# Attention in 64x64 tiles of the PE array, q and k transposed by DMA, and w_out matmuls 14 slots behind those of w_in

## The chip, the core and the metric

The kernel runs on one core of a Trainium2 chip. Its engines work side by side, each on its own instruction stream: TensorE (PE, matmuls, with a weight-load part PEld), VectorE (DVE), ScalarE (ACT), GpSimd (POOL) and SyncE (SP). Matmul results go to PSUM, which has eight banks of 512 float32 columns; everything else lies in SBUF. DMAs are issued here by POOL (loads) and by SP (stores). The metric is the device time of one execution in microseconds (us); lower is better.

## What is computed

```python
# q, k, v: (8 batches, 8 heads, 576 tokens, 64)
scores = q @ k.T / sqrt(64), only where |i - j| <= 32
attn = softmax(scores);  a = attn @ v
x = a.transpose(0, 2, 1, 3).reshape(4608, 512)
h = x @ w_in                      # w_in 512 x 2048
g = where(h >= 1, h, where(h <= -1, 0, (h + 1)**2 / 4))
out = g @ w_out                   # w_out 2048 x 512, out float32
```

Inputs are float32; the kernel works in bfloat16 and sums in float32.

## The kernel before

**Order.** The order of the instructions is written out by hand. A prelude computes the first half of batch 0's attention. Then one loop of 152 slots (index `a`, `t` the block of 256 tokens, `f` one of eight pieces of 256 columns of w_in) carries the rest. A slot holds, on PE, eight matmuls of 256 columns with w_in (L359, result `hp`); ACT then computes `rr` (L363), DVE `tensor_max` in place in `hp` (L364) and the product `gT` (L365), which together are the activation. `hp` has two PSUM banks. Four matmuls of 512 columns with w_out (L375, result `op`) follow for the block before, eight slots behind; every fourth slot an `op` bank is finished, copied by ACT to `osb` (L379) and stored by SP (L381). Slots 0 to 7 have no w_out matmuls, slots 144 to 151 nothing but them.

**Attention in the slots.** Heads go in pairs: head y in partitions 0 to 63, head y+4 in 64 to 127; there are four such pairs a batch, 32 in all (index `i`). A dictionary `ev` says which piece of attention sits in which slot. `relay` (L171) reorders a loaded q; `tpose` transposes q or k on PE (L187) and copies the result out of PSUM, for q to `qT` (L200, ACT), for k into the block-diagonal buffer `kz` (L194, mostly DVE, partly ACT in the first slots). `kz` holds, for each chunk of 64 keys, the two heads' columns in separate halves with zeros elsewhere, so that one full 128x128 matmul computes both heads. `scores` runs nine such matmuls for an index in three groups (L220), takes the exponential on ACT (L224) and multiplies by the window mask on DVE (slots below 16) or POOL (L225). `pv` runs twice for an index, for 288 queries each: row sums with a block-diagonal matrix of ones (`dn`, L238 and L239), products with block-diagonal `vz` (`nm`, L248), then reciprocal as Ln and Exp on ACT (L252, L253); the product of both (L257, DVE) writes `xT`, the operand of the w_in matmuls, at the beginning of the next slot (`flush`).

**Loads.** All loads are issued by POOL and cast float32 to bfloat16. For q rows of 2,304 bytes are read (L100); for k (from the third double pair on) and v pieces of 256 bytes (L95, L105), one double pair (`m`, two indices) at a time. The prelude issues the loads of the first three double pairs and all weights; those of the fourth and later stand at the head of given slots. A load waits for the eighth load before it in this queue.

Of the kernel before, what the change touches and what calls it, by code (L numbers as in the profile page):

```python
# [8 lines left out]
FP = mybir.dt.float32  # L9
# [6 lines left out]
def kernel(  # L16
# [15 lines left out]

    nc = tc.nc
    B, H, S, D = q.shape
    NT, DM, DFF = out.shape[0], 512, 2048
    NP = B * H // 2
    NC = S // 64
    HALF = S // 2

    def qrange(c):  # L40
        return max(0, 64 * c - 32), min(S, 64 * c + 96)


    GROUPS = [(0, 2, 4), (1, 3), (6, 8, 5, 7)]
    pcol, PW = {}, 0
    for c in (1, 3, 0, 2, 4, 6, 8, 5, 7):
        pcol[c] = PW
        PW += qrange(c)[1] - qrange(c)[0]

    def pc(c, qq):  # L50
        return pcol[c] + qq - qrange(c)[0]

    const = ctx.enter_context(tc.tile_pool(name="const", bufs=1))
    qkn = ctx.enter_context(tc.tile_pool(name="qkn", bufs=3))
    qjp = ctx.enter_context(tc.tile_pool(name="qjp", bufs=2))
    qtp = ctx.enter_context(tc.tile_pool(name="qtp", bufs=3))
    ptp = ctx.enter_context(tc.tile_pool(name="ptp", bufs=4))
# [11 lines left out]
    ones2 = const.tile([128, 128], BF, name="ones2")  # L69
    mask1 = const.tile([128, 128], BF, name="mask1")  # L70
    maskp = const.tile([128, PW], BF, name="maskp")
    w_in = const.tile([128, 4, DFF], BF, name="w_in")
    w_out = const.tile([128, 16, DM], BF, name="w_out")
    zrow = const.tile([128, 2 * S], BF, name="zrow")
    xT = const.tile([128, 4, NT], BF, name="xT")
    kz = [const.tile([128, NC, 2, 64], BF, name=f"kz{i}") for i in range(6)]
    vz = [const.tile([128, 2, NC, 128], BF, name=f"vz{i}") for i in range(4)]

    ctx.enter_context(tc.manual_schedule())


    qn, kn = {}, {}

    LONG = 2

    def load_qk(m):
        b, qd = divmod(m, 2)
        for src, dst, nm in ((q, qn, "qn"), (k, kn, "kn")):  # L90
            if nm == "kn" and m >= LONG:
                t = dst[m] = qkn.tile([128, NC, 2, D], BF, name="kn", tag="kn")
                for g in range(2):
                    for h in range(2):
                        nc.gpsimd.dma_start(out=t[64 * g:64 * g + 64, :, h],  # L95
                                            in_=src[b, 2 * qd + g + 4 * h].rearrange("(c r) d -> r c d", r=64))
                continue
            t = dst[m] = qkn.tile([128, 2, S], BF, name=nm, tag=nm)
            rows = src[b].rearrange("(h y) s d -> h (y s) d", h=2)[:, 2 * qd * S:2 * qd * S + 2 * S]
            nc.gpsimd.dma_start(out=t, in_=rows.rearrange("h (x j) d -> x h (j d)", j=NC))  # L100

    def load_v(m):
        b, qd = divmod(m, 2)
        for h in range(2):
            nc.gpsimd.dma_start(  # L105
                out=vz[m % 4][64 * h:64 * h + 64, :, :, 64 * h:64 * h + 64].rearrange("r g c d -> r (g c) d"),
                in_=v[b, 4 * h + 2 * qd:4 * h + 2 * qd + 2].rearrange("g (c r) d -> r (g c) d", r=64))
# [7 lines left out]
    def load_w_out(n):  # L115
        nc.gpsimd.dma_start(out=w_out[:, 8 * n:8 * n + 8],
                            in_=moe_w_out.rearrange("(ko ki) f -> ki ko f", ki=128)[:, 8 * n:8 * n + 8])

    nc.scalar.preload_act_table_set("natural_log_exp_and_others")
    load_qk(0)  # L120
# [9 lines left out]
    load_qk(1)  # L130

    def vz_off(n, h):
        return vz[n][64 * h:64 * h + 64, :, :, 64 * (1 - h):64 * (1 - h) + 64].rearrange("r g c d -> r (g c) d")

    nc.vector.memset(zrow, 0.0)
    for n in range(2):
        for h in range(2):
            nc.scalar.copy(vz_off(n, h), zrow[64 * h:64 * h + 64].rearrange("r (c d) -> r c d", d=64))
    for t in kz:
        for h in range(2):  # L140
            nc.vector.memset(t[64 * h:64 * h + 64, :, 1 - h], 0.0)
    nc.vector.memset(ones2, 0.0)
    for h in range(2):
        nc.vector.memset(ones2[64 * h:64 * h + 64, 64 * h:64 * h + 64], 1.0)
    for cs in ((0,), (2, 4, 6), (8,), (1, 3), (5, 7)):
        q0, q1 = qrange(cs[0])
        j0 = q0 - (64 * cs[0] - 32)
        n = len(cs)
        nc.vector.tensor_copy(
            maskp[:, pcol[cs[0]]:pcol[cs[0]] + n * (q1 - q0)].rearrange("p (n j) -> p n j", n=n),  # L150
            mask1[:, j0:j0 + q1 - q0].rearrange("p (n j) -> p n j", n=1).to_broadcast([128, n, q1 - q0]))
    load_v(0)
    load_v(1)
    load_w_in(0, 512)
    load_w_in(512, DFF)
    for n in (2, 3):
        for h in range(2):
            nc.gpsimd.memset(vz_off(n, h).bitcast(FP), 0.0)
    load_qk(2)
    load_v(2)  # L160
    load_w_out(0)
    load_w_out(1)


    qj, kj, qT, kT = {}, {}, {}, {}

    def relay(m, t, eng):

        src, dst, nm = ((qn, qj, "qj"), (kn, kj, "kj"))[t]
        dst[m] = qjp.tile([128, NC, 2, D], BF, name=nm)  # L170
        eng.tensor_copy(dst[m].rearrange("p j h d -> p h j d"),  # L171
                        src[m].rearrange("p h (j d) -> p h j d", d=D))

    TJ = [(0, 5), (5, 9)]

    def tpose(m, t, early=False):

        nat = t >= 2 and m >= LONG
        src = qj if t < 2 else kn if nat else kj
        dst = qT if t < 2 else kT  # L180
        j0, j1 = TJ[t % 2]
        if t % 2 == 0 and not nat:
            dst[m] = qtp.tile([128, 2, S], BF, name="qT" if t < 2 else "kT")
        pool, tag = (ps_h, "hp") if early else (ps_s, "sc")
        ps = pool.tile([128, 5, 128], BF, name="tp", tag=tag)
        for j in range(j0, j1):
            nc.tensor.transpose(ps[:, j - j0], src[m][:, j].rearrange("p h d -> p (h d)"), ident)  # L187
        n = j1 - j0
        if nat:
            for g in range(2):  # L190
                for h in range(2):
                    r = slice(64 * h, 64 * h + 64)
                    copy = nc.scalar.copy if m < 4 and h else nc.vector.tensor_copy
                    copy(kz[2 * (m % 3) + g][r, j0:j1, h],  # L194
                                          ps[r, :n].rearrange("d c (g r) -> d g c r", g=2)[:, g])
            return
        o = dst[m].rearrange("d g (p j) -> d g p j", j=NC)[:, :, :, j0:j1]
        i = ps[:, :n].rearrange("d j (g p) -> d g p j", g=2)
        if t < 2 or t == 3:
            nc.scalar.copy(o, i)  # L200
        else:
            nc.vector.tensor_copy(o, i)

    def zfill(m, g, early=False):
        for h in range(2):
            r = slice(64 * h, 64 * h + 64)
            copy = nc.gpsimd.tensor_copy if not early else nc.scalar.copy if h else nc.vector.tensor_copy
            copy(kz[2 * (m % 3) + g][r, :, h], kT[m][r, g].rearrange("d (c r) -> d c r", r=64))

    pt = {}  # L210

    def scores(i, g, eng):
        m, gg = divmod(i, 2)
        if g == 0:
            pt[i] = ptp.tile([128, PW], BF, name="pt")
        ps = ps_s.tile([128, 512], FP, name="sc", tag="sc")
        off = 0
        for c in GROUPS[g]:
            q0, q1 = qrange(c)
            nc.tensor.matmul(ps[:, off:off + q1 - q0], kz[2 * (m % 3) + gg][:, c].rearrange("d h r -> d (h r)"),  # L220
                             qT[m][:, gg, q0:q1], start=True, stop=True)
            off += q1 - q0
        seg = slice(pcol[GROUPS[g][0]], pcol[GROUPS[g][0]] + off)
        nc.scalar.activation(pt[i][:, seg], ps[:, :off], AF.Exp, scale=D ** -0.5)  # L224
        eng.tensor_mul(pt[i][:, seg], pt[i][:, seg], maskp[:, seg])  # L225

    def pv(i, hf, spare=False):
        lo, hi = HALF * hf, HALF * hf + HALF
        if spare:
            dn = ps_o.tile([128, HALF], FP, name="dn", tag="op")  # L230
            nm = ps_o.tile([128, HALF], FP, name="nm", tag="op")
        else:
            dn = ps_d.tile([128, HALF], FP, name="dn")
            nm = ps_n.tile([128, HALF], FP, name="nm")
        odd = (1, 3) if hf == 0 else (5, 7)
        e0 = pc(2 * hf * 2, lo) if hf else pc(0, 0)
        o0, o1 = qrange(odd[0])[0], qrange(odd[1])[1]
        nc.tensor.matmul(dn, ones2, pt[i][:, e0:e0 + HALF], start=True, stop=False)  # L238
        nc.tensor.matmul(dn[:, o0 - lo:o1 - lo], ones2, pt[i][:, pcol[odd[0]]:pcol[odd[0]] + o1 - o0],  # L239
                         start=False, stop=True)  # L240
        parts = []
        for c in list(range(0, NC, 2)) + list(range(1, NC, 2)):
            q0, q1 = qrange(c)
            q0, q1 = max(q0, lo), min(q1, hi)
            if q0 < q1:
                parts.append((c, q0, q1))
# [58 lines left out]
    TB = 256  # L305
# [115 lines left out]
```

## Time and profile before

Three runs took 357.29, 357.70 and 357.76 us, median 357.70. The profiled execution took 357.66 us, of which the profile's span is 355.8; about 1.9 us lie outside the span.

| | busy, us | share of the span | instructions |
|---|---|---|---|
| PE | 322.8 | 91% | 2752 |
| PEld | 233.0 | 65% | 2752 |
| DVE | 272.8 | 77% | 513 |
| ACT | 227.7 | 64% | 455 |
| POOL | 166.5 | 47% | 211 |

| groups | count | mean, ns |
|---|---|---|
| hp matmul, 256 columns (L359) | 1152 | 275 |
| op matmul, 512 columns (L375) | 576 | 379 |
| sc / dn / nm matmuls (L220, L238 and L239, L248) | 288 / 128 / 320 | 220 / 285 / 215 |
| transposes on PE (L187) | 288 | 236 for q |
| rr on ACT (L363) | 144 | 596 |
| hp, gT on DVE (L364, L365) | 144 each | 699, 687 |
| exp on ACT (L224), 480 / 352 / 256 columns | 32 each | 564 / 459 / 379 |
| mask on POOL (L225), 480 / 352 / 256 columns | 26 / 24 / 24 | 1094 / 874 / 682 |
| Ln, Exp of the sums (L252, L253), 288 columns | 64 each | 414, 444 |
| kz copies on DVE (L194), 320 / 256 columns | 52 / 52 | 319 / 286 |
| xT on DVE (L257), 288 columns | 64 | 455 |
| osb copy on ACT (L379) | 36 | 586 |

Matmuls are pipelined: the mean of one is its latency, longer than its distance from the next, so a matmul's price is read from the starts of a run of them. In the timeline a row is a run of like instructions: start, length, engine, line, operation, operands and count. In the table of stages each engine's busy time in the stage is followed by its number of instructions; the last three numbers are the granted clock, the DMA share and GB/s. A line of the waits reads: engine and line, what it waited for, us in total, times, longest. A line of the chain: start, length, what it was.

### The profile page before, as it was taken

Reading aid. Unit: us, or ns where it says so; the run is one execution under the profiler, and the core shown is the slowest. Engines: PE = TensorE matmul, PEld = TensorE weight load, DVE = VectorE, ACT = ScalarE, POOL = GpSimd, SP = SyncE. Lnnn points to the kernel's source line nnn. Section 1 sums busy time; section 2 is a strip of 40 time slices with the busy share of each in tenths; the row PEclk is TensorE's granted clock in tenths of the full one; section 3 lists DMA queues with packets and bytes.
Section 4 is the critical chain, followed back from the end, with each engine's and each line's share of the span. In section 5 each row is a group of like instructions: output and inputs, shape, how many; then the busy total and the mean of one; then the engine's idle time right before and its main releaser. Section 6 shows DMA issues by size and latency. Waiting matters only on the chain.

```text
span 355.8 us, 7157 instructions
## 1 busy us (share of the span) xinstructions
PE 322.8 (91%) x2752; PEld 233.0 (65%) x2752; DVE 272.8 (77%) x513; ACT 227.7 (64%) x455; POOL 166.5 (47%) x211
## 2 busy tenths in 40 slices
PE   1768197878999999999999999999999999999995
PEld 1647174655777777777777777777777776666662
DVE  7549368676888888888888888888888787887770
ACT  6977366676777777777777777777766654444441
POOL 8946393068494849494949494942423300000000
PEclk9989889999999999999999999999999999999999
DMA  7999999059693939393939393930000000010011
GB/s 106 185 201 193 185 169 133 2 60 101 64 88 74 88 72 91 71 89 71 91 71 96 65 98 64 97 65 31 31 31 31 29 30 31 31 59 29 32 46 72
DMA packets 83809, 28.24 MB, mean 79 GB/s; under 512 B 71488, under 2 KB 78656, under 8 KB 83776
## 3 DMA queue, kind: packets, MB, share of 16 engines
q0 software_dynamic: 78592, 18.36, 56.3%
q1 hardware_dynamic: 5184, 9.44, 7.1%
q8 instruction: 21, 0.34, 0.4%
q14 instruction: 12, 0.10, 0.1%
HBM read 36.70 MB, written 9.44 MB: 130 GB/s over the span
## 4 chain that ended last, share of the span: by engine, by line
PE 79%; DMA 8%; DVE 5%; POOL 3%; ACT 3%; issue 2%; ACTq 0%; POOLq 0%
PE op L375 33%; PE hp L359 32%; DMA qn<-in_q_dram 4%; DMA w_in<-in_moe_w_in_dram 4%; PE nm L248 4%; PE tp L187 3%; PE sc L220 3%; PE dn L238 2%; PE dn L239 2%; DVE hp L364 1%; DVE gT L365 1%; DVE kz L194 1%; POOL vz L105 1%; ACT rr L363 1%; ACT kz L194 1%
## 5 line engine op out<-in xcount | busy, mean ns | idle before, releaser
L359 PE MATMUL hp<-xT,w_in 128*128 128x256 bf16 x1152 | 151.7, 275 | 1.6 <-DVE gT L365 1.2
L375 PE MATMUL op<-w_out,gT 128*128 128x512 bf16 x576 | 146.5, 379 | 0.0
L363 ACT ACTIVATE rr<-hp 128x512 f32<-128x512 f32 x144 | 85.8, 596 | 72.7 <-PE hp L359 69.8
L364 DVE TENSOR_TENSOR hp<-hp,rr 128x512 f32<-128x512 f32 x144 | 100.7, 699 | 40.9 <-ACT rr L363 38.0
L359 PEld LDWEIGHTS <-w_in 128*128 128x128 bf16 x1152 | 109.2, 99 | 21.6 <-DVE gT L365 1.9
L225 POOL TENSOR_TENSOR pt<-pt,maskp 128x480 bf16<-128x480 bf16 (+2 forms) x74 | 65.6, 889 | 101.9 <-ACT pt L224 101.7
L365 DVE SCALAR_TENSOR_TENSOR gT<-rr,hp 128x512 bf16<-128x512 f32 x144 | 98.9, 687 | 4.9
L375 PEld LDWEIGHTS <-gT 128*128 128x128 bf16 x576 | 53.0, 98 | 37.2
L224 ACT ACTIVATE pt<-sc 128x352 bf16<-128x352 f32 (+2 forms) x96 | 44.3, 468 | 0.7 <-PE sc L220 0.6
L95 POOL DMA_DIRECT2D kn<-in_k_dram x56 | 41.8, 775 | 1.0 <-DVE qj L171 0.9
L257 DVE TENSOR_TENSOR xT<-nm,rc 128x288 bf16<-128x288 f32 x64 | 29.0, 455 | 14.1 <-ACT rc L253 12.3
L220 PE MATMUL sc<-qT,kz 128*128 128x128 bf16 (+1 forms) x288 | 30.9, 220 | 5.5 <-ACT pt L224 4.3
L252 ACT ACTIVATE lr<-dn 128x288 f32<-128x288 f32 x64 | 26.5, 414 | 13.7 <-PE dn L239 13.6
L194 DVE COPY kz<-tp 64x320 bf16<-64x320 bf16 (+1 forms) x104 | 31.4, 302 | 2.8 <-ACT kz L194 1.8
L200 ACT COPY qT<-tp 128x640 bf16<-128x640 bf16 (+1 forms) x32 | 23.5, 741 | 12.7 <-PE tp L187 9.7
L105 POOL DMA_DIRECT2D vz<-in_v_dram x32 | 28.3, 897 | 4.8 <-DMA w_out<-in_moe_w_out_dram 2.9
L253 ACT ACTIVATE rc<-lr 128x288 f32<-128x288 f32 x64 | 28.4, 444 | 2.0
L187 PE MATMUL tp<-ident,qj 128*128 128x128 bf16 x144 | 14.4, 236 | 16.8 <-DVE qj L171 9.7
L220 PEld LDWEIGHTS <-kz 128*128 128x128 bf16 x288 | 23.3, 100 | 8.6 <-issue 5.4
L248 PE MATMUL nm<-pt,vz 128*128 128x128 bf16 (+2 forms) x320 | 26.6, 215 | 2.1 <-DVE xT L257 2.0
L379 ACT COPY osb<-op 128x512 f32<-128x512 f32 x36 | 21.1, 586 | 10.2 <-PE op L375 7.8
L187 PEld LDWEIGHTS <-qj 128*128 128x128 bf16 x144 | 11.3, 106 | 23.3 <-DVE qj L171 16.6
(39 smaller groups left out, 163.0 us busy)
## 6 DMA issues: line engine op xcount, KB each, us to landing
out_dram<-osb SPq DMA_DIRECT2D x36, 256.0 KB, 2.0
qn<-in_q_dram POOLq DMA_DIRECT2D x16, 288.0 KB, 4.3
vz<-in_v_dram POOLq DMA_DIRECT2D x32, 144.0 KB, 4.9
kn<-in_k_dram POOLq DMA_DIRECT2D x56, 72.0 KB, 4.0
w_out<-in_moe_w_out_dram POOLq DMA_DIRECT2D x2, 1024.0 KB, 11.8
w_in<-in_moe_w_in_dram POOLq DMA_DIRECT2D x2, 768.0 KB, 11.4
kn<-in_k_dram POOLq DMA_DIRECT2D x2, 288.0 KB, 4.8
w_in<-in_moe_w_in_dram POOLq DMA_DIRECT2D x2, 256.0 KB, 6.4
```

The costliest lines, as they stand in the source:

```text
L95: nc.gpsimd.dma_start(out=t[64 * g:64 * g + 64, :, h], in_=src[b, 2 * qd + g + 4 * h].rearrange("(c r) d -> r c d", r=64))
L187: nc.tensor.transpose(ps[:, j - j0], src[m][:, j].rearrange("p h d -> p (h d)"), ident)
L194: copy(kz[2 * (m % 3) + g][r, j0:j1, h], ps[r, :n].rearrange("d c (g r) -> d g c r", g=2)[:, g])
L220: nc.tensor.matmul(ps[:, off:off + q1 - q0], kz[2 * (m % 3) + gg][:, c].rearrange("d h r -> d (h r)"), qT[m][:, gg, q0:q1], start=True, st ...
L224: nc.scalar.activation(pt[i][:, seg], ps[:, :off], AF.Exp, scale=D ** -0.5)
L225: eng.tensor_mul(pt[i][:, seg], pt[i][:, seg], maskp[:, seg])
L248: nc.tensor.matmul(nm[:, q0 - lo:q1 - lo], vz[i // 2 % 4][:, i % 2, c], pt[i][:, pc(c, q0):pc(c, q0) + q1 - q0], start=n == 0, stop=n == l ...
L359: nc.tensor.matmul(hp[:, j], w_in[:, kk, 256 * f + 128 * j:256 * f + 128 * j + 128], xT[:, kk, TB * t:TB * t + TB], start=kk == 0, stop=kk ...
L363: nc.scalar.activation(rr, hp, AF.Relu, scale=0.5, bias=0.5)
L364: nc.vector.tensor_max(hp, hp, rr)
L365: nc.vector.scalar_tensor_tensor(gT[t][:, 2 * f:2 * f + 2], rr, 1.0, hp, op0=ALU.min, op1=ALU.mult)
L375: nc.tensor.matmul(op, gT[t - 1][:, ff, 128 * tt:128 * tt + 128], w_out[:, ff], start=ff == 0, stop=ff == 2 * NF - 1)
```

## The change

The heads' pairing, the activation and the tiling of the two large matmuls stay. What becomes different:

- **Tiles of the PE array.** Every attention matmul takes 64 rows (one head's 64 features, or 64 keys) and writes 64 partitions. No operand is block-diagonal any more: `kz`, `vz`, their zero fills and `zfill` go. `scores` issues 16 matmuls of 128 queries for an index (eight chunks of keys, two heads) into two PSUM banks, one for each head; `scores8` does the last, ninth chunk of all four indices of a batch together. `pv` is one pass of 480 queries in two phases, `pv8` one of 96 queries for the four indices of a batch. In the first phase `nm` takes keys of one row half while `dn` takes those of the other; the second phase exchanges them. Between the phases DVE copies one element of the bank (`part`), so that the second phase waits for the first.
- **Transposes.** Only batch 0 is still transposed on PE, in the prelude. For all other batches `xpose` issues one DMA transpose for q and one for k from SP, from SBUF to SBUF.
- **Loads.** `load_nat` loads q, k or v of a whole batch with two DMAs of 2,304 rows of 256 bytes; batch 1 is loaded whole before w_out, later ones from slots 10 (b = 2) and 18 (b - 2) + 1 on. w_out is loaded by four DMAs instead of two.
- **Order.** w_out matmuls come 14 slots (`LAG`) behind those of w_in instead of eight; the loop has 158 slots. In a slot with attention the order on PE is hp, first phase of a `pv`, `scores` of a later index, second phase, op. `xT` becomes a ring of four batches.

```diff
+    def load_nat(b, t):
+        src, dst, nm = ((q, qn, "qn"), (k, kn, "kn"), (v, vn, "vn"))[t]
+        x = dst[b] = nat.tile([128, NU, 2, D], BF, name=nm, tag=nm, bufs=3 if t == 2 else 2)
         for h in range(2):
+            nc.gpsimd.dma_start(out=x[:, :, h], in_=src[b, NY * h:NY * h + NY].rearrange("y s d -> (y s) d")
+                                .rearrange("(u p) d -> p u d", p=128))
...
+    def xpose(b, t):
+
+        if t == 1:
+            kT[b] = ktp.tile([128, NY * S], BF, name="kT")
+        o = qT(b) if t == 0 else kT[b]
+        nc.sync.dma_start_transpose(out=o.rearrange("d (u p) -> d u p", p=128),
+                                    in_=(qn, kn)[t][b].rearrange("p u h d -> p (u h d)"))
...
+    def scores(i, eng):
+        b, y = divmod(i, NY)
+        p = pt[i] = ptp.tile([128, 2, 512], BF, name="pt")
+        ps = [ps_s.tile([128, 512], FP, name="sc", tag="sc") for _ in range(2)]
+        for c in range(8):
+            for h in range(2):
+                nc.tensor.matmul(ps[h][half(NC * y + c), 128 * (c // 2):128 * (c // 2) + 128],
+                                 kT[b][HD[h], S * y + 64 * c:S * y + 64 * c + 64],
+                                 qTs[b % 3][HD[h], PAD + S * y + 64 * c - 32:PAD + S * y + 64 * c + 96],
+                                 start=True, stop=True)
         for h in range(2):
+            nc.scalar.activation(p[:, h], ps[h], AF.Exp, scale=D ** -0.5)
+            eng.tensor_mul(p[:, h], p[:, h], mask4)
...
+    def part(ps, col):
+
+        nc.vector.tensor_copy(scr[64:65, 0:1], ps[64:65, col:col + 1])
...
+    def pv(i, lo=0, hi=MAIN, alt=False):
+
+        b, y = divmod(i, NY)
+        nm, dn = banks(alt)
+        def sums(par, first):
+            R = half(y + par)
...
+                    yield lambda h=h, c2=c2, a0=a0, a1=a1, n=n: mm(
+                        nm[HD[h], a0 - lo:a1 - lo], vn[b][R, (NC * y + 2 * c2 + par) // 2, h],
+                        pt[i][R, h, a0 + 32 - 64 * par:a1 + 32 - 64 * par],
+                        start=first and n == 0, stop=not first)
...
+        def rows(par, first):
+            R = half(y + par)
+            a0 = max(lo, 32 * par)
+            for h in range(2):
+                yield lambda h=h: mm(dn[HD[h], a0 - lo:hi - lo], ones[R],
+                                     pt[i][R, h, a0 + 32 - 64 * par:hi + 32 - 64 * par], start=first, stop=not first)
+
+        def phase(first):
+            s = list(sums(0 if first else 1, first))
+            if not first:
+                s.reverse()
+            for f in s[:2] + list(rows(1 if first else 0, first)) + s[2:]:
+                f()
+            if first:
+                part(nm, hi - lo - 1)
...
+    LAG = 14
...
+    at(9, [], ("m", 4))
+    at(10, [], ("m", 5))
+    at(11, [("m", 4)], ("m", 6))
+    at(12, [("m", 5)], ("m", 7))
+    at(13, [("m", 6)], ("t", 1))
+    at(14, [("m", 7)], None)
+    at(17, [("t", 1)], ("m", 8))
+    sl = [20, 23, 26, 29]
+    sl += [33, 36, 39, 42, 45]
+    sl += [50, 54, 59, 63, 68]
+    sl += [72, 75, 78, 81, 84]
+    sl += [88, 91, 94, 98, 102]
+    sl += [105, 108, 111, 114, 117, 122]
...
+    loads, xps = {}, {7: [(1, 0)], 8: [(1, 1)]}
     for b in range(2, B):
+        a = 10 if b == 2 else 18 * (b - 2) + 1
+        for t in range(3):
+            loads.setdefault(a + t, []).append((b, t))
+        for t in range(2):
+            xps.setdefault(a + (5 if b == 2 else 8) + t, []).append((b, t))
...
+        if not sc:
+
+            for x in pvs:
+                x[0]()
         if t < NB:
             if f == 0:
-                gT[t] = gtp.tile([128, 2 * NF, TB], BF, name="gT")
-            hp = ps_h.tile([128, 2, TB], FP, name="hp")
+                gT[t] = gtp.tile([128, 2 * NF, TB], BF, name="gT", tag="gT")
+            r0 = TB * t % RING
+            hp = ps_h.tile([128, 2, TB], FP, name="hp", tag="hp")
...
+        if sc:
+            for x in pvs:
+                x[0]()
+        if t < NB:
 
             rr = ewp.tile([128, 2, TB], FP, name="rr")
             nc.scalar.activation(rr, hp, AF.Relu, scale=0.5, bias=0.5)
             nc.vector.tensor_max(hp, hp, rr)
             nc.vector.scalar_tensor_tensor(gT[t][:, 2 * f:2 * f + 2], rr, 1.0, hp, op0=ALU.min, op1=ALU.mult)
...
+        if sc:
+            (scores if sc[0] == "m" else scores8)(sc[1], eng)
+        for x in pvs:
+            x[1]()
+        for x in pvs:
+            x[2]()
+        if a >= LAG:
+            for x in range(4 * (a - LAG), 4 * (a - LAG) + 4):
...
+        for x in xps.get(a, []):
+            xpose(*x)
```

In `ev`, "m" is one index, "t" the ninth chunks of a batch; `sl` lists the slots of batches 2 to 7, each with the `pv` of one entry and the `scores` of the next. `x[0]`, `x[1]` and `x[2]` are the two phases and the end (Ln, Exp and the xT product of the next slot).

## The prediction

> **What bounds the kernel now.** I read, in this order: the slice table, a table of stages, the PE timeline of one slot with attention and one without, then waits and chain of the early stage. The page's slices (40 of 8.9 us each):
>
> ```profile
> PE   1768197878999999999999999999999999999995
> PEclk9989889999999999999999999999999999999999
> ```
>
> PE is full from slice 10 on and has holes before. The table of stages (us, PE, weight loads, DVE, ACT, POOL, clock, DMA, GB/s), cut where the picture changes:
>
> ```profile
> 0.00:21.90 21.90, 10.09 (x84) 8.05 (x85) 13.73 (x42) 17.64 (x30) 18.59 (x34) 0.97 1.20 158
> 21.90:84.70 62.80, 45.37 (x423) 33.65 (x421) 42.45 (x89) 38.78 (x85) 32.35 (x42) 0.93 1.19 126
> 84.70:284.30 199.60, 199.60 (x1796) 147.15 (x1793) 167.10 (x310) 142.35 (x292) 115.31 (x137) 1.00 0.60 70
> 284.30:344.20 59.90, 59.90 (x423) 40.79 (x422) 47.68 (x71) 26.56 (x46) 0.26 (x1) 1.00 0.10 36
> 344.20:355.80 11.60, 7.80 (x37) 3.33 (x34) 1.82 (x3) 2.35 (x4) 0.00 (x0) 0.97 0.18 68
> ```
>
> Three regimes: a prelude; 63 us in which PE has slack (45.4 of 62.8); then 260 us in which PE never rests, DVE 84% busy. A slot of the loop (eight hp matmuls, four op matmuls) without attention, from the PE timeline:
>
> ```profile
> 292.83 1.04 PE L359 MATMUL hp<-xT,w_in 128*128 128x256 bf16 x8
> 293.71 1.03 PE L375 MATMUL op<-w_out,gT 128*128 128x512 bf16 x4
> 294.57 1.04 PE L359 MATMUL hp<-xT,w_in 128*128 128x256 bf16 x8
> ```
>
> From start to start: 1.74 us a slot, 0.87 for each half, so 0.42 ns a streamed column (0.865/2048). Pace of attention:
>
> ```profile
> 228.60 0.40 PE L248 MATMUL nm<-pt,vz 128*128 128x64 bf16 x5
> 228.84 1.04 PE L359 MATMUL hp<-xT,w_in 128*128 128x256 bf16 x8
> ```
>
> Five matmuls (128, 128, 96, 128 and 64 columns, 544 in all) pass in 0.24 us: 48 ns each, 0.44 ns a column. Loading weights costs nothing on top; streaming is the price. The early stage, in waits and chain:
>
> ```profile
> PE tp L187 <- ACT kz L194: 7.5, 2, 7.2
> POOL qn L100 <- DMA w_out<-in_moe_w_out_dram: 4.5, 1, 4.5
> ...
> 28.28 13.92 DMA qn<-in_q_dram
> ```
>
> PE stands 7.2 us before slot 7, because the q of the fourth pair of heads, issued at 28.3, sits behind w_out in the DMA engines until 42.2. By the PE timeline the hp matmuls of slots 0, 14 and 19 start at 21.9, 64.2 and 84.7: slots 14 to 19 take 4.1 us each. The chain of 64 to 84.7 us runs mostly over DVE and ACT (kz copies, gT, hp, rc, lr): that many evacuations in these slots are late, with PE waiting.
>
> **What the Trainium skill says.** "TensorEngine Tiling (Array Packing)", Tiling Modes: tiles may load weights and multiply in parallel, but changing the mode drains TensorE. The same page, Restrictions: column tiling takes Fast Weight Load away. "TensorE: Matmul & The Clock Gate", Part 1: matmuls never start less than about 25 ns apart, however small. "DMA: Bandwidth & Descriptors", Latency and other measured facts: a DMA transpose moves 261 GB/s. The trace of before has only 128x128 matmuls and no DMA transpose, so it shows none of these; it agrees as far as 48 ns a matmul lies above the 25.
>
> **The change part by part.**
>
> *Tile matmuls.* Before, attention streams 34,816 columns each for scores, dn and nm and 36,864 for transposes (288 x 128): 141,312 columns, 59.4 us at 0.42. After, one group (scores and pv of one index) is 16 matmuls of 128 and 20 of 64 to 480 columns (3,712 for pv); over four tiles 512 + 928 = 1,440 column times, 0.60 us. A tail group (scores8 and pv8) has 8 + 32 matmuls, 832 column times, 0.35 us. If issue at 25 ns decides, 36 x 25 = 0.90 and 40 x 25 = 1.00 us. From slot 14 on there are 24 groups, 6 tail groups and one pv8: 24 x 36 + 6 x 40 + 32 = 1,136 matmuls. Bounds: 16.8 us (pure streaming, 24 x 0.60 + 6 x 0.35 + 0.27) and 54.5 (48 ns each, today's pace with no overlap). I take 25 ns, the skill's floor as an estimate, because a phase of pv (eight 128-column products on one row half beside two long sums on the other) streams for 0.22 us, about the 0.25 which ten issues need: 28.4 us.
>
> *Changes of mode.* Phase 1, scores and phase 2 stand together between hp and op matmuls, so two changes a slot, 31 slots. A drain is no more than a matmul's shown duration less its spacing (a 256-column matmul lasts 0.275 and is spaced 0.109, so 0.17); lower bound near 0.05. I take 0.125 each: 31 x 2 x 0.125 = 7.8 us (3.1 to 10.5).
>
> *The added wait.* `part` (a one-element DVE copy) waits for phase 1, and phase 2 for it. Behind it on DVE are this slot's hp and gT steps, so a late phase 1 delays the release of the hp buffer, for which the hp matmuls two slots on wait. That loop is 0.87 + 0.60 + 0.70 + 0.69 and signals, some 3.1 us for two slots of 3.5: covered alone. In a slot with attention ACT has two exps (by L224, 590 ns each) and Ln and Exp of 480 columns (about 0.6 each) ahead of the next rr, and DVE a longer xT product (0.65); then it is just late. Today hp waits 1.2 us for gT in all. I take 4 us (0 to 8; a gain is excluded, as nothing on PE gets shorter by it). `part` itself is covered by the scores matmuls between the phases.
>
> *Copies and memsets removed.* On DVE 104 kz copies (31.4 us), on ACT most qT copies (23.5), on POOL ten relays (11.4). In the full stage they lie beside PE and give nothing by themselves; they count in slots 0 to 19, and as DVE room for `part`. POOL's loads fall from 106 to 48 issues for q, k and v. By 775 ns for 576 rows and 897 for 1,152, one of 2,304 rows costs about 1.14 us; 6 a batch fit between the masks (two of 512 columns, 1.15 us each), whose results pv wants three slots later.
>
> *Loads and DMA transposes.* Rows of 256 B grow from 69,000 to 101,000. A burst of 4,608 such rows and a long q passes today in about 8 us; a batch has 13,824, so 22 to 24 us in 18 slots (36 us): covered, but q is no longer free of small rows. Each transpose moves 590 KB: 2.3 us by the skill's rate, plus 2 as a plain DMA takes to land; it queues on SP behind the out stores, which it can hold up in turn. From load to first score there are 14 slots, 28 us; loads of q and k take 15, so transposes up to 6 us each cost nothing. For batch 1 all loads now precede w_out (11.8 us to land), so what landed at 42 lands by about 31, and transposed by 40; slot 9, which scores first, comes at 41. The 7.2 us hole goes; next late is DVE. If a transpose costs 5 us more, slot 9 is 8 to 10 us later.
>
> *w_out six slots later.* Four op matmuls a slot, the osb copy on ACT and the store on SP all start at slot 14 rather than 8. Slots 0 to 13 then have no op work and are DVE's: 14 x 1.386 = 19.4; masks on DVE 4 x 0.84 + 0.5; xT products 4.3; `part` 0.8: 28.3 us, with a tenth for the waits between ACT and DVE 31. Six op quartets move to the end, 6 x 0.865 = 5.2 us.
>
> *Sum against the profiled span.* To slot 0: 21.0 (21.9 less a microsecond, since the relay, today at 7.47, waited for kz and maskp set-up on DVE). Slots 0 to 13: 31. Slots 14 to 143: 130 x 1.737 = 225.8. Tile matmuls 28.4, mode changes 7.8, waits 4. Last 14 quartets 12.1. Tail 3.8, as 352.0 to 355.8 today. Sum 333.9. The median of the runs is 357.7 for a span of 355.8, so 1.9 on top: 335.8, **336**. Against before: slot 19 would come near 62 instead of 84.7, 5.2 are owed at the end, and the slots from 19 on get 4 shorter (today 258.7 for 124 slots, 215.4 of it plain work, so 43.3 of attention; after, 40.2 less slot 17's share of 1.4).
>
> **Rivals.**
> *Full overlap.* Four tiles stream at 13 ns a matmul, mode changes cost 0.05, no stalls: 16.8 + 3.1 in place of 40.2, so 316. For it: the skill's parallel tiles, weights hidden today. Against: its own 25 ns floor.
> *ACT and DVE keep the early stage.* Slots 14 to 19 show 4.1 us when evacuations pile up; if slots 0 to 19 again run 0.5 us longer each, or transposes come late for batch 1, 10 us are lost: 346 (340 to 357). For it: each group still needs 2.4 us of ACT. Against: no kz copies any more.
> *Slower: weight loads show.* Each tile matmul brings its own load, without the fast form. If load and matmul take turns, at today's 48 ns or more, D grows by 1,136 x 23 ns = 26 us: 362. It turns to slower at 25 + (357.7 - 336)/1.136 = 44 ns. For it: 1,504 small pairs replace 736 of scores, dn and nm. Against: 128-column loads hide wholly today.
> *The tiles don't overlap at all.* Then a group streams 2,048 + 3,712 columns, 2.4 us, a tail group 1.4: 24 x 2.4 + 6 x 1.4 + 1.1 = 67 us for 28.4: 375. This is the change not doing what it says.
>
> **How the numbers follow.** Forecast 0.47 (own range 324 to 347, from 20 to 32 ns, the drains and 0 to 8 of stalls), full overlap 0.15, early stage 0.17, weight loads 0.15, no overlap 0.06. Within 0.2% (0.7 us, about what a measurement can tell from no change) lies 0.02 of the early-stage case; slower is 0.15 + 0.06 = 0.21, faster the other 0.77. From 314 to 360 leaves out no overlap, most of the weight-load case and the lowest part of full overlap, about 0.19.
>
> **What would show it.** The spacing of sc and nm matmuls (25 ns, or 13, or 48); slots with attention 2.8 us long, others 1.74; slot 14 near 52 us; PE waits before sc of batch 1 on a DMA into kT or qT small; PE waiting for gT a few us in all. The forecast falls if op matmuls don't begin by 56 us, or if a group adds over 1.6 us to its slot.

## The result and the profile after

The changed kernel takes 363.07 us (median of four, 360.82 to 363.71) against 357.73 for the one before: 1.014 times as long, 95% interval 1.0092 to 1.0187. The forecast was 336. The profiled execution took 363.69 us, its span 362.0. Executions over 1.5% above the fastest of their kernel are counted as slow and left out of the ratios; only the first experiment has any (six of twenty).

The table of stages of the changed kernel, cut at the beginning of slot 0, the end of slot 9's w_in matmuls, the first scores of batch 1 and slot 14 (us, then PE, weight loads, DVE, ACT, POOL, clock, DMA, GB/s; the DMA share adds up the times of all packets, so it passes 1 where packets overlap):

```profile
0.00:27.00 27.00, 11.34 (x177) 7.97 (x178) 12.71 (x33) 11.90 (x23) 18.82 (x29) 1.00 1.32 159
27.00:50.30 23.30, 16.14 (x157) 10.39 (x156) 14.27 (x27) 9.05 (x19) 5.12 (x5) 1.00 1.94 147
50.30:66.70 16.40, 0.09 (x5) 0.04 (x8) 1.72 (x3) 0.60 (x1) 3.63 (x3) 0.62 2.13 117
66.70:82.30 15.60, 10.15 (x175) 6.98 (x176) 11.19 (x24) 10.21 (x20) 0.00 (x0) 0.83 2.00 148
82.30:300.00 217.70, 208.71 (x2334) 141.44 (x2368) 167.89 (x269) 136.09 (x252) 97.14 (x90) 0.99 0.92 99
```

The third row is a stage in which PE has next to nothing to do (0.09 of 16.4 us) and the DMA engines are full: the hole. The waits name its cause, and the chain goes straight through two transfers:

```profile
PE sc L178 <- DMA kT<-kn: 17.1, 2, 16.3
```

```profile
12.71 17.75 DMA qn<-in_q_dram
30.54 7.34 SPq L162
38.00 28.62 DMA kT<-kn
66.66 0.64 PE sc L178 x14
```

The q of batch 1 lands at 30.5 and its transpose is issued. The k has landed by 34.5, but SP is still issuing q's transpose; k's follows at 38.0, and kT is there only at 66.6. The scores of slot 9 wait from 50.3.

From slot 14 on the total comes close to the forecast. In the PE timeline of a slot with attention:

```profile
107.98 1.04 PE L400 MATMUL hp<-xT,w_in 128*128 128x256 bf16 x8
108.95 0.23 PE L199 MATMUL nm<-pt,vn 64*64 64x96 bf16 x2
108.95 0.38 PE L199 MATMUL dn<-pt,ones 64*64 64x448 bf16 x2
109.02 0.33 PE L199 MATMUL nm<-pt,vn 64*64 64x128 bf16 x6
109.17 0.40 PE L178 MATMUL sc<-qT,kT 64*64 64x128 bf16 x16
109.63 0.22 PE L199 MATMUL nm<-pt,vn 64*64 64x64 bf16 x2
...
110.84 0.38 PE L400 MATMUL hp<-xT,w_in 128*128 128x256 bf16 x2
```

From hp to hp it is 2.86 us, so a group adds 1.12 to the 1.74 of a plain slot; the forecast had 0.90 of issue, 0.25 of mode changes and 0.13 of waits, 1.28. Sixteen score matmuls take 0.40 us, one alone 0.216 (the shortest of this tile), so they start (0.40 - 0.216)/15 = 12 ns apart. At 0.42 ns a column one tile alone would need 54 ns a matmul (an estimate), so the four overlap fully.

Against the sum on record, in us:

| | forecast | measured (span) | difference |
|---|---|---|---|
| to slot 0 | 21.0 | 27.0 | +6.0 |
| slots 0 to 13 | 31 | 55.3 | +24.3 |
| from slot 14 to the end | 281.9 | 279.7 | -2.2 |
| sum | 333.9 | 362.0 | +28.1 |

Of the 24.3, 16.3 are the hole. What remains is 8 us in slots 0 to 13 that the forecast had too short.

### The profile page after: what moved, and what is told of

Same layout as the page of the kernel before. It is cut to its first block, busy times and chain, and to the rows that moved or that the text cites. A ratio compares the mean times of both kernels' runs of the same rounds, so it can differ in the third digit from the quotient of the medians.

```text
span 362.0 us, 7810 instructions
## 1 busy us (share of the span) xinstructions
PE 303.8 (84%) x3227; PEld 202.6 (56%) x3268; DVE 245.1 (68%) x410; ACT 190.6 (53%) x353; POOL 124.7 (34%) x127
## 4 chain that ended last, share of the span: by engine, by line
PE 62%; DMA 14%; POOL 9%; DVE 5%; issue 4%; ACT 3%; SPq 2%; ACTq 0%; POOLq 0%
PE op L422 29%; PE hp L400 27%; DMA kT<-kn 9%; DMA qn<-in_q_dram 5%; PE nm L199 4%; SPq L162 2%; POOL vn L91 2%; POOL pt L184 2%; DVE hp L409 2%; POOL qn L91 2%; ACT rr L408 2%; DVE gT L410 1%; POOL kn L91 1%; DVE scr L205 1%; PE dn L199 1%
## 5 line engine op out<-in xcount | busy, mean ns | idle before, releaser
L184 POOL TENSOR_TENSOR pt<-pt,mask 128x512 bf16<-128x512 bf16 x48 | 54.6, 1161 | 117.0 <-ACT pt L183 117.0
L183 ACT ACTIVATE pt<-sc 128x512 bf16<-128x512 f32 x64 | 34.7, 594 | 22.8 <-PE sc L178 22.6
L199 PE MATMUL nm<-pt,vn 64*64 64x128 bf16 (+2 forms) x656 | 33.8, 224 | 15.4 <-DVE xT L222 11.7
L199 PEld LDWEIGHTS <-vn 64*64 64x64 bf16 x656 | 24.0, 113 | 27.7 <-issue 25.5
L222 DVE TENSOR_TENSOR xT<-nm,rc 128x480 bf16<-128x480 f32 (+3 forms) x44 | 25.8, 592 | 19.7 <-ACT rc L221 15.6
L199 PE MATMUL dn<-pt,ones 64*64 64x64 bf16 (+5 forms) x272 | 33.1, 304 | 1.1 <-DVE xT L222 0.4
L221 ACT ACTIVATE rc<-lr 128x480 f32<-128x480 f32 (+3 forms) x44 | 24.3, 552 | 1.4
L178 PEld LDWEIGHTS <-kT 64*64 64x64 bf16 x512 | 12.4, 116 | 20.6 <-DMA kT<-kn 17.5
L220 ACT ACTIVATE lr<-dn 128x480 f32<-128x480 f32 (+3 forms) x44 | 23.1, 525 | 0.3
L91 POOL DMA_DIRECT2D kn<-in_k_dram x14 | 17.1, 1232 | 14.3 <-DMA vn<-in_v_dram 13.8
L91 POOL DMA_DIRECT2D vn<-in_v_dram x16 | 19.6, 1239 | 3.9 <-DMA w_out<-in_moe_w_out_dram 3.7
```

The source lines that it names most:

```text
L91: nc.gpsimd.dma_start(out=x[:, :, h], in_=src[b, NY * h:NY * h + NY].rearrange("y s d -> (y s) d") .rearrange("(u p) d -> p u d", p=128))
L178: nc.tensor.matmul(ps[h][half(NC * y + c), 128 * (c // 2):128 * (c // 2) + 128], kT[b][HD[h], S * y + 64 * c:S * y + 64 * c + 64], qTs[b % ...
L183: nc.scalar.activation(p[:, h], ps[h], AF.Exp, scale=D ** -0.5)
L184: eng.tensor_mul(p[:, h], p[:, h], mask4)
L199: return nc.tensor.matmul(o, w, x, skip_group_check=True, **kw)
L221: nc.scalar.activation(rc[:, :n], lr[:, :n], AF.Exp, scale=-1.0)
```

## The experiments

Two theories from the trace: the transposes are slow because other loads share the DMA engines with them (A: batch 2's loads, which POOL issues early; B: w_out and the rest of batch 1), or the early chain of PE, ACT and DVE would be as late without them.

**Batch 2's loads held back.**

```diff
+            if x == (2, 0):
+                nc.gpsimd.tensor_copy(scrp[0:1, 0:1], kT[1][0:1, 0:1])
             load_nat(*x)
```

> The changed kernel, but POOL reads one element of batch 1's kT before it issues the loads of batch 2, so these come after both transposes of batch 1. Theory A (the two transposes of batch 1 are slow because batch 2's loads share the DMA engines with them): kT lands by about 48 us instead of 66.6, the 16.3 us hole before the scores of slot 9 shrinks below 3, and the time falls to about 349; some of it may come back as a wait for batch 2 near slot 17. Theory B (w_out and the rest of batch 1 crowd them, batch 2's loads hardly): kT still lands after 58 us and the time stays within 3 us of 363.

The median of the twenty executions is 357.65 us (354.16 to 363.70), that of the fourteen that count 356.9; ratio to before 0.9952 (0.993 to 0.9973). In the profiled one (357.80 us) kT lands at 60.2 and the hole is 9.8 us. The landing fits B, the time neither theory. kT comes 6.4 us earlier, of which 0.9 was there before any load of batch 2 could act (q lands at 29.5 instead of 30.5); the rest of the delay remains. With twenty executions spread over 9.5 us this share is no firm number.

**w_out held back too**, its loads and batch 2's after the transposes of batch 1.

```diff
-    for n in range(4):
-        load_w_out(n)
...
+    xpose(1, 0)
+    xpose(1, 1)
+    nc.gpsimd.tensor_copy(scrp[0:1, 0:1], kT[1][0:1, 0:1])
+    for n in range(4):
+        load_w_out(n)
     A = nc.scalar.copy
```

> As the kernel that holds batch 2's loads, and w_out's four loads too are issued only after both transposes of batch 1. Theory A: kT lands by about 45 us, no better for the hole than holding batch 2 alone, and w_out, landing near 58, makes slot 14 wait: some 352 to 356. Theory B: only this kernel removes the hole; kT lands by 45 us, and the time is 350 to 356, below that of the kernel that holds batch 2 alone.

352.18 us, ratio 0.9831 (0.9791 to 0.9871). The time lies in both ranges; what tells the theories apart is where kT lands and whether the hole is there. SP's timeline of the changed kernel and of this one (start, time in issue):

```profile
30.54 7.34 SPq L162 DMA_TRANSPOSE qT<-qn  x1
38.00 17.60 SPq L162 DMA_TRANSPOSE kT<-kn  x1
```

```profile
29.62 5.50 SPq L160 DMA_TRANSPOSE qT<-qn  x1
35.23 6.63 SPq L160 DMA_TRANSPOSE kT<-kn  x1
```

The same transfer, issued three microseconds apart, keeps SP 17.6 or 6.6 us, and kT lands at 66.6 or 44.6. PE's wait on kT at slot 9 is gone; the longest one on kT that is left, 2.5 us, is for batch 2's at slot 17. So, taken away in this order, w_out has the larger share (15.6 of the 22 us), batch 2's loads the smaller; w_out held back alone was not run. With both gone the transposes of q and k still take 12.1 and 9.4 us, beside the last loads of batch 1. The wait for w_out at slot 14, which A's expectation named, did not come: op begins at 67.7, and each of the loads took 13 us at most.

**Batch 1 transposed on PE**, so that the first DMA transposes are batch 2's. `ptpose` transposes five or four natural 128x128 pieces into an `sc` bank, and ACT copies them.

```diff
+        for u in range(u0, u1):
+            nc.tensor.transpose(ps[:, u - u0], (qn, kn)[t][b][:, u].rearrange("p h d -> p (h d)"), ident)
+        o = qT(b) if t == 0 else kT[b]
+        copy(o[:, 128 * u0:128 * u1], ps[:, :u1 - u0].rearrange("d u p -> d (u p)"))
...
-    loads, xps = {}, {7: [(1, 0)], 8: [(1, 1)]}
+    loads, xps = {}, {}
```

> Only batch 1 is transposed on PE again, 36 transposes with eight ACT copies of about 0.75 us in slots 2 to 8, in place of two DMA transposes. Theory A and B alike (the hole is the late DMA transpose): no PE wait on kT at slot 9, kernel at 345 to 348, since 16.3 us of hole and about 2 us of half clock after it go. Rival C (the early stage is bound by ACT and DVE anyway, and what the hole gives is lost again in slots 10 to 17, for instance on batch 2): 355 to 361.

349.50 us, ratio 0.9768 (0.9726 to 0.981): 13.6 us below the changed kernel, against 15 to 18 expected. In the traces slot 14 begins 15.9 us earlier; about 1 us of that is lost again by slot 17 and the rest after slot 40, which was not followed up. Slots 11, 12 and 13 stay long: 3.2, 3.8 and 6.7 us from start to start, against 2.9, 3.5 and 6.2 in the changed kernel. With this alone the change is faster than the kernel before.

The same trace shows what the transposes do to the loads. From issue to landing (shortest, median, longest) the four loads of w_out take, in the changed kernel and in this one:

```profile
DMA to landing us min/median/max: 30.0/31.2/32.0
DMA to landing us min/median/max: 16.4/17.0/18.0
```

Batch 2's loads stand behind them in both. Without the two DMA transposes the last piece of w_out lands at 48.3 instead of 62.9. Two transfers that take about 4.6 us each when little else runs thus hold up the loads by 14.6 us: the delay is mutual.

**Only the first phases of slots 0 to 2 moved** behind their w_in matmuls, the hole left as it is.

```diff
-        if not sc:
+        if not sc and a > 2:
...
-        if sc:
+        if sc or a <= 2:
             for x in pvs:
                 x[0]()
```

> Only the first phases of pv in slots 0 to 2 are moved behind the w_in matmuls of their slots, so that these no longer stand behind the wait for the xT product. If the hole hides everything ahead of it (kT lands at 66.6 us whatever PE does before): within 1 us of 363, with the hole longer by what slots 0 to 2 gain, about 4 us. If the early chain counts by itself: 358 to 360.

363.08 us, ratio 1.0159 (1.0116 to 1.0203), as expected of a hole that hides everything ahead of it. Slot 9's w_in matmuls begin at 44.2 instead of 49.3, and the wait for kT grows from 16.3 to 19.8 us (kT lands at 65.0 here): what the early chain gains, the hole takes.

**The same edit where there is no hole** (with batch 1 on PE; slot 14 included).

```diff
-        if not sc:
+        if not sc and t >= NB:
...
-        if sc:
+        if t < NB:
             for x in pvs:
                 x[0]()
```

> Batch 1 transposed on PE, and in all slots the first phase of pv stands behind the w_in matmuls (that concerns slots 0 to 2 and 14). Theory (the DMA hole hid the early chain; without the hole it counts): what moving the phases could not give alone it gives now, 3 to 5 us below the 349.5 of the kernel with PE transposes, 345 to 347. Rival (the next DMA, batch 2's loads and transposes near slot 17, is due right behind): 348.5 to 350.5.

343.39 us, ratio 0.9595 (0.955 to 0.964): 6.1 below the 349.50, more than expected. The profiled executions (350.13 and 341.84) differ by 5.1 us at slot 13, 4.5 of it by slot 3: that is the edit which gave nothing beside the hole. Another 3.1 come at slot 14, whose first phase the run with the hole had not moved; what that is worth there was not tried.

**Banks in turn up to slot 13** (with batch 1 on PE).

```diff
-        pvs = [pv(*e[1:], alt=a < 3) if e[0] == "m" else pv8(e[1], alt=a < 3) for e in pvs]
+        pvs = [pv(*e[1:], alt=a < 14) if e[0] == "m" else pv8(e[1], alt=a < 14) for e in pvs]
```

> Batch 1 transposed on PE, and pv in slots 3 to 13 takes its banks in turn from the two pairs that slots 0 to 2 use, since op needs none before slot 14. Theory (slots 11 to 14 take 3.3 to 6.7 us because phase 1 of one pv waits for the xT product of the one before, through Ln and Exp): waits of PE for xT fall from 10.8 us to about 6 and the time to 345 to 347. Rival (ACT and DVE themselves are full there): 348.5 to 350.5, with the wait under another name.

345.78 us, ratio 0.9668 (0.9632 to 0.9704). PE's waits for xT fall from 10.8 to 6.7 us, and slots 11 to 14 now take 3.2, 2.9, 3.1 and 3.3 us. The chain from the second phase over Ln, Exp and xT to the next first phase was a cause of the long slots 11 to 14.

**Both**, the two last edits together, with batch 1 on PE.

> All three: batch 1 on PE, first phases behind w_in, banks in turn up to slot 13. If the two gains add, 340 to 343; if a later wait for batch 2 or ACT and DVE take over, 344 to 348.

343.28 us, ratio 0.9587 (0.954 to 0.9633): no different from the first phases moved alone. Waits for xT are down to 2.1 us, but those for `part` rise from 3.0 to 5.5. The gains don't add; the time falls between the two ranges of the expectation.

**w_out eight slots behind** with batch 1 on PE and the first phases moved.

```diff
-    LAG = 14
+    LAG = 8
```

> Batch 1 on PE, first phases behind w_in, and w_out eight slots behind w_in as before the change, not 14. If PE has room in slots 8 to 13 (DVE bounds them): the six quartets, 5.2 us, come out of the end and the time is 3 to 5 us below the kernel with the same two edits and 14 slots. If the order on PE is what bounds these slots (each quartet delays the next phase): within 1.5 us of it.

342.60 us, ratio 0.9576 (0.9551 to 0.96), 0.8 below the same kernel with 14 slots, which is nothing that can be told apart. That is the second range of the expectation, but not for the reason given there: slot 17 waits 5.9 us for batch 2's kT. SP's timeline (in a row of two, from the first issue to the end of the second):

```profile
53.81 11.77 SPq L440 DMA_DIRECT2D out_dram<-osb  x2
65.69 2.88 SPq L162 DMA_TRANSPOSE qT<-qn  x1
68.67 2.72 SPq L162 DMA_TRANSPOSE kT<-kn  x1
```

With 14 slots the same transposes are issued at 53.3 and 60.1, before any store. With eight, two output stores stand ahead of them on SP, and the second waits for slot 15's op.

**Batch 2 on PE as well**, eight slots. `ptp_at` lists the slots of the PE transposes (batch, q or k, part), and `xpose` begins with batch 3.

```diff
+    ptp_at = {2: [(1, 0, 0)], ..., 13: [(2, 0, 0), (2, 0, 1)], 14: [(2, 0, 2), (2, 0, 3)],
+              15: [(2, 1, 0), (2, 1, 1)], 16: [(2, 1, 2), (2, 1, 3)]}
...
-        for t in range(2):
+        for t in range(2) if b > 2 else ():
             xps.setdefault(a + (5 if b == 2 else 8) + t, []).append((b, t))
```

> Eight slots for w_out, first phases behind w_in, and batch 2 as well as batch 1 transposed on PE (slots 13 to 16). With eight slots PE waited 5.9 us for batch 2's kT at slot 17. If it is the DMA transpose that is late there, this wait goes and the time is 337 to 339, against 342.6. If it is the load of k that is late, PE waits for kn instead, in slots 15 and 16, and the time is 341 to 344.

336.22 us, ratio 0.9395 (0.9381 to 0.9409), the fastest of all and just below the expected range: the wait of 5.9 us is gone and PE waits for no kn, so it was the transpose behind the stores. Slices of PE and clock (40 of 8.4 us):

```profile
PE   1567797999999999999999999999999999999995
...
PEclk9999999999999999999999999999999999999999
```

From slot 0 on (24.5 us) PE is busy for 70% or more of every slice but the last, and the clock column shows full speed throughout.

**All batches on PE**, otherwise as with both early edits: `ptp_at` goes on with eight parts a batch from slot 18 (b - 2) + 7 on, and no `xpose` is left.

> The kernel with all three edits (343.3), but every batch is transposed on PE, none by DMA: 216 more PE transposes and 48 more ACT copies in the full stage. If DMA transposes are worth their place there, PE's 216 x 0.053 = 11.5 us come on top: 354 to 356. If PE has gaps that take the transposes (DVE and ACT waits): 344 to 349.

349.32 us, ratio 0.9761 (0.9747 to 0.9776), 6.0 above the kernel that leaves batches 2 to 7 to DMA, and just above the second range. But PE has no gaps that take the transposes:

```profile
84.28 0.44 PE L173 MATMUL tp<-ident,qn 128*128 128x128 bf16 x5
84.56 1.04 PE L413 MATMUL hp<-xT,w_in 128*128 128x256 bf16 x8
```

Five push back the next w_in matmuls by 0.28 us, 56 ns each, and against the kernel with both edits the 30 slots with the transposes of batches 3 to 7 are 10.1 us longer in all, the full price of 180. What is won back lies in two slots of that kernel, slot 14 (1.1 us longer there) and above all slot 50, which takes 6.2 us there and 2.8 here, because there batch 4's transposes stand behind the store of slot 45:

```profile
110.50 18.39 SPq L440 DMA_DIRECT2D out_dram<-osb  x3
129.05 2.53 SPq L162 DMA_TRANSPOSE qT<-qn  x1
131.68 3.02 SPq L162 DMA_TRANSPOSE kT<-kn  x1
138.18 0.64 PE L190 MATMUL sc<-qT,kT 64*64 64x128 bf16 x16 [2.38 <-DMA kT<-kn]
```

So a DMA transpose that lands in time saves PE its whole price; the 6.0 us are that price less what late ones cost. With eight slots for w_out no transpose of batches 3 to 7 makes PE wait.

**The changed kernel with eight slots, nothing else** (`LAG = 8`).

> The changed kernel with w_out eight slots behind w_in, nothing else. If the DMA hole decides (66.6 us for kT, and w_out itself landing at 53 to 62 us), the earlier op matmuls only wait inside the same hole, and what they save at the end is at most 5.2 us less what they add in slots 10 to 13: 359 to 363. If 14 slots were themselves a cause of the loss: below 358.

367.07 us, ratio 1.0284 (1.0229 to 1.034): slower than both expectations. PE waits 4.0 us for w_out at slot 8 and 10.0 for kT at slot 9, and 6.5 more for batch 2's kT at slot 17, which is issued behind the stores:

```profile
36.47 18.70 SPq L162 DMA_TRANSPOSE kT<-kn  x1
76.28 12.36 SPq L427 DMA_DIRECT2D out_dram<-osb  x2
88.75 2.80 SPq L162 DMA_TRANSPOSE qT<-qn  x1
```

In the changed kernel batch 2's q transpose is issued at 68.6. The 14 slots are thus no cause of the loss; with batch 2's transposes on SP they keep it smaller.

**The kernel before with its fourth double pair loaded ahead of w_out.**

```diff
     load_v(2)
+    load_qk(3)
+    load_v(3)
     load_w_out(0)
...
-    loads = {0: [(load_qk, 3), (load_v, 3)]}
+    loads = {}
```

> The kernel before, with the loads of its fourth double pair moved ahead of w_out's. If its 7.2 us hole at slot 7 is the order of the loads alone, q no longer comes late, w_out comes 5 us later and is wanted at slot 8: 351 to 355. If the late transposes, kz copies and slots of 4.1 us after the hole decide the early stage, the gain is given back: 356 to 358.

355.19 us, ratio 0.9927 (0.9913 to 0.9942), just above the first range. The hole of 7.2 us becomes 4.2. This order of loads alone is worth 2.7 us in the kernel before, so it does not account for the 21.6 us between that kernel and the fastest version, the change with its early stage repaired. Other repairs of the kernel before were not tried.

## Why the prediction was wrong

Step by step, as it was put:

- *Tile matmuls, 28.4 us at 25 ns.* Too dear. Scores start 12 ns apart; phase 1, scores and phase 2 stream for about 0.22, 0.20 and 0.22 us (phase 2 taken like phase 1), 0.64 where the forecast had 0.90. "TensorEngine Tiling (Array Packing)", Tiling Modes, of the Trainium skill is borne out (tiles work in parallel); the floor of 25 ns in "TensorE: Matmul & The Clock Gate", Part 1, does not hold between different tiles. The rival of full overlap had this term right (13 ns) but not the rest; the weight-load rival and the one without overlap fell. The count is short by the `pv` of slot 14: 20 matmuls, 0.5 us at 25 ns, and two changes of mode.
- *Changes of mode, 0.25 us a group.* About right. From the last hp to phase 1 0.10 us pass, and of the group's 1.12 us some 0.2 are left for both changes together.
- *"`part` itself is covered by the scores matmuls", all waits 0.13 us a group.* Wrong: this wait alone is twice that. From the end of the scores to phase 2 0.26 us pass without a change of mode. Slot 26 as shown above, with its copy on DVE, and slot 29, where `scores8` has half the matmuls:

```profile
109.42 0.16 DVE L205 COPY scr<-nm 1x1 f32<-1x1 f32 x1
115.50 0.26 PE L191 MATMUL sc<-qT,kT 64*64 64x96 bf16 x8
115.75 0.16 DVE L205 COPY scr<-nm 1x1 f32<-1x1 f32 x1
115.96 0.22 PE L199 MATMUL nm<-pt,vn 64*64 64x64 bf16 x2 [0.20 <-DVE scr L205]
```

  In both, phase 2 starts 0.46 us after the scores and 0.05 after the copy ends, and both slots are equally long to 0.01 us: the copy decides, not the number of score matmuls. (It starts just after phase 1 and after DVE's gT of the slot before; these end 0.03 us apart, so which of them it waits for is open.) In 31 groups that makes some 8 us (an estimate from 0.26). The errors have opposite signs; that the sum from slot 14 on is only 2.2 us off is in part luck.
- *Loads of batch 1.* "Lands by about 31": q does, at 30.5; the k lands at 34.5 and the v at 50.2.
- *DMA transposes: "transposed by 40; slot 9 ... comes at 41. The 7.2 us hole goes".* This is the step that failed. The price taken for a transpose, an estimate of 2.3 us by the skill's rate ("DMA: Bandwidth & Descriptors", Latency and other measured facts) and 2 to land, fits one that runs in the full stage: 4.6 us in the shortest case, 5.1 and 5.5 as medians. In the early stage q took 20.7 and k 28.6 us, and k's could be issued only when SP was through with q's. With w_out and batch 2's loads out of the way k took 9.4: the price had no term for what else is in the DMA engines. Nor had the loads a term for the transposes: w_out landed after 31 us, against 11.8 in the kernel before and 17 with batch 1 on PE. The prediction had a dearer transpose only as a case of 5 us more.
- *Batch 2's loads.* The change puts them at slot 10, and the prediction has nothing for them before that. POOL has no mask to compute before slot 16 and waits for no slot, so it issued the first of them at 32.4 us, when PE was in slot 1. A slot orders the instructions of one engine; it is no time for an engine that waits for nothing in it. With these loads held back kT came 6.4 us earlier.
- *Slots 0 to 13, 31 us by DVE's sum plus a tenth, after 21.0 for the prelude.* The sum is nearly what these slots take without the hole and the chains: 32.5 us (24.5 to 57.0) with batch 1 on PE, the first phases moved and the banks in turn, against 39.4 with batch 1 on PE alone. In the changed kernel slots 0 to 2 wait for xT ahead of w_in, and slots 11 to 14 for the one pair of `nm` and `dn` banks; a sum of busy times has no term for such chains, which are most of the 8 us beside the hole. The w_in matmuls at half speed in slots 0 to 3 lie in the same stretch and were not separated. The prelude was mis-sized: slot 0 came at 27.0, and at 24.5 with the first phases behind w_in; the other 3.5 us have no cause shown.
- *w_out six slots later.* Right that 5.2 us move to the end: from the start of slot 143 to the end of the span it is 17.6 us with 14 slots and 12.4 with eight (batch 1 on PE, first phases moved). What was named in the text (stores and transposes share SP) counts both ways: 14 slots avoid it for batch 2 and meet it for batch 4, at slot 50.
- *Rivals.* "*ACT and DVE keep the early stage* ... or transposes come late for batch 1, 10 us are lost" had the right place at less than half the size: the total is 28.1 us above the sum, which is beyond that rival's range of 340 to 357.

Shown by the runs: the hole is the late DMA transpose of batch 1, made late by w_out and other loads. Repaired by PE transposes for batches 1 and 2 and by the order of the first phases, with w_out at eight slots, the same design takes 336.2 us. That this equals the forecast is luck: slot 0 comes at 24.5 instead of 21.0, slots 0 to 13 take 35.3 instead of 31, and the rest 274.6 instead of 281.9.

## What to carry to other kernels

Price a transfer by what is in the DMA engines when it runs, find that from when its issuing engine is free, not from the place of its line in the program, and count what the transfer does to the others. When one wait ends last in a stage, improvements ahead of it show nothing until it is gone: moving the first phases of slots 0 to 2 gave 0 us with the hole and about 5 without. A queue that carries both stores and transfers that the next stage needs (SP here) ties their order to the order of the stores. A small instruction that only keeps an order can cost more than its own length: here 0.26 us a group.

## What the runs showed of the hardware that was not expected

- Matmuls in 64x64 tiles at different positions of the array start 12 ns apart (scores, slot 26), though each has its own weight load.
- A DMA transpose of 590 KB between SBUF places lands in 4.6 us beside nothing but an output store, and in 28.6 with loads of small rows and w_out beside it; it holds SP for 2.7 or 17.6 us. Two of them beside these loads delay the loads by 14.6 us.
- Matmuls ran at half speed from the start of the changed kernel to slot 3, although the clock column says 1.00. The eight w_in matmuls of slots 0, 1 and 2 take 1.82 us to the next matmul; in slot 26 the same takes 0.97 (107.98 to 108.95).

```profile
26.98 1.89 PE L400 MATMUL hp<-xT,w_in 128*128 128x256 bf16 x8
28.80 0.26 PE L199 MATMUL nm<-pt,vn 64*64 64x64 bf16 x2
```

  Just after the hole they take 1.82 us as well, and there the column says 0.50. Neither the cause nor why the column does not show the first stretch was tested.
